# Clustered attention and two MLPs on one core: operands of the first head pair written by ACT and DVE, centroids masked, the first scores split, idle matmuls placed

## The chip, the cores and the metric

One core of a Trainium2 chip. The metric is the device time of one execution in microseconds (us). PE is TensorE, DVE is VectorE, ACT is ScalarE, POOL is GpSimd, SP is SyncE, which here only issues DMAs.

## What is computed

```python
# q, k, v: (2 batches, 8 heads, 768 tokens, 64); centroids: (8, 16, 64)
q_assign = argmax(q_n @ c_n.T)          # nearest of 16 centroids, by cosine
k_assign = argmax(k_n @ c_n.T)
mask   = q_assign[..., :, None] == k_assign[..., None, :]
scores = where(mask, 0.125 * q @ k.T, -1e9)
attn   = softmax(scores)
x = (attn @ v) reshaped to (1536, 512)
x = max(max(x @ w1, x @ w2), x @ w3) @ w_out      # width 768
h = x @ w_in;  out = max(0.01 * h, h) @ w_out2    # width 2048
```

## The kernel before

Attention runs first, then both MLPs. The 16 heads of the two batches are taken as 8 pairs; a pair's q and k stand transposed in SBUF as 128 x 768 (`rq`, `rk`, head 0 in partitions 0 to 63, head 1 in 64 to 127). A unit is 256 query rows of one head, six units a pair, 48 in all.

Every float32 product is made from a high part (rounded to fp32r) and a low rest. For one head the score operands are four tiles: q1 holds the high part of q over its low part, k1 the high part of k twice, q2 the high part of q over 16 rows that tell q's cluster, k2 the low part of k over 16 rows that hold 0 or -2^100 by k's cluster. The sum q1.k1 + q2.k2 is then the masked score. In `scores` (L534) 128 query rows of a unit take four matmuls at L543: two (512 and 256 columns) with q1 and k1 over 128 rows, two with q2 and k2 over 80 rows, all into one of two PSUM buffers. `maxima` (L548) is the row maximum on DVE, `exps` (L553) the exponential with its row sum on ACT; after it the PSUM buffer is free. `transposes` (L585, L593) turns the exponentials on PE, `out_of_psum` and `rests` split them, `values` (L627, L638) multiplies them by v.

For a pair's operands `round_q` and `round_k` (L380, L385) write the high parts of both heads in one 128-row tile, `rest_q` and `rest_k` (L390, L395) the low ones, and `operands` (L500, L504) copies half tiles by DMA on SP's queue into q1, q2, k1, k2: six copies a head, each 64 x 768, and two small ones for the cluster rows. Clusters come from `sims` (L417, L421: six products of 128 tokens with 32 centroid columns, twelve matmul records), `near_max`, `near_eq`, `weigh`, `first_max` and `first_eq` (L432 to L472: five short steps on DVE that give a one-hot of the first maximum), and a transposition of the one-hot on PE: `onehot_T` (L479), or for head 0 of the first pair `onehot_up` (L488), from where CQ (L849, ACT) and CK (L854 on DVE, then L857 on ACT) bring the 16 rows into q2 and k2.

The order of every engine's work is written out by hand. `BEGIN` (L53) is a list of steps that is emitted first, `ORDER` (L37) the six lists that repeat for the units, `END` (L60) the last. A step "S0:1" is score half 0 of unit 1, "G0@1" the q side of `sims` for pair 1, "I2" is `idle(WARM[2])`. `idle(n)` (L786) emits n bf16 matmuls of 128 x 512 zeros into a PSUM tile that nothing reads. WARM is (8, 2, 3, 4): 8 at the start, 2 after the centroids' transposition, 3 at I2.

The beginning, with what the steps stand for: load centroids, rq, rk; scale the centroids to length one and write the result twice side by side (L809), transpose (L811), copy the two 64 x 64 halves into `cb` that was cleared before (L794, L814), so that a pair's head 0 meets only its own 16 columns and head 1 its own; G0@0, G1@0 (clusters of pair 0), G0@1, UQ, idle, G1@1, UK, CK; S0:0, S1:0 (the first scores); OT (one-hots for head 1), S0:1, S1:1, T0:0 and so on. D0a and D0b are the DMA copies of heads 0 and 1 of pair 0; D2 is head 1's cluster rows.

Of the kernel before, what the change touches and what calls it, by code (L numbers as in the profile page):

```python
# [8 lines left out]
F32 = mybir.dt.float32  # L9
# [8 lines left out]
P = 128  # L18
# [32 lines left out]
)  # L51

BEGIN = (  # L53
# [4 lines left out]
)  # L58

END = (  # L60
# [13 lines left out]
}  # L74
WAYS = ("DPP", "DDP", "DPA", "DDP", "DDP", "DPA")
ENGINE = {"QH": "A", "QH@1": "P", "KH": "P", "VH": "P", "KL": "P", "KL@0": "D", "VL": "P", "W": "P", "W@1": "D"}
WARM = (8, 2, 3, 4)
PACE = 0.16
FIRST = ("G0", "G1", "N0a", "N0b", "N1a", "N1b", "W", "QH", "KH", "QL", "LD")
SPARE = {"G0": (4, 0), "G1": (5, 0), "O0": (2, 0), "O1": (3, 0)}  # L80
# [7 lines left out]
def clustered_attention_mlps(  # L88
# [229 lines left out]
    with ExitStack() as att:  # L318
# [92 lines left out]
        def bank():  # L411

            st["bank"] = st.get("bank", -1) + 1
            ps = ps_s.tile([P, 1024], F32, tag="s", name=f"s{st['bank']}")
            return ps[:, 0:S], ps[:, S:1024]
# [84 lines left out]
        def operands(p, part, heads=(0, 1), queue=nc.sync):  # L500
# [5 lines left out]
            for j in heads:  # L506
# [12 lines left out]
                else:  # L519
# [3 lines left out]
                    if part != 1:  # L523
                        dma(q2[D : D + C], s["oo"][j * C : (j + 1) * C])
                        dma(k2[D : D + C], s["oo"][(2 + j) * C : (3 + j) * C])

        un = {}

        def unit(n):
# [1 line left out]
            j, g = divmod(r, NG)  # L531
            return p, j, g

        def scores(n, i):  # L534
            p, j, g = unit(n)
            q1, q2, k1, k2 = st[p][j]
            if i == 0:
                un[n] = {"e": [], "sum": sums[n % len(sums)]}
            c0 = g * G + i * P
            ps, spare = bank()  # L540
            for a, b, start in ((q1, k1, True), (q2, k2, False)):
                for lo, hi in ((0, 512), (512, S)):
                    nc.tensor.matmul(  # L543
                        ps[:, lo:hi], a[:, c0 : c0 + P], b[:, lo:hi], start=start, stop=not start
                    )
            un[n]["s", i], un[n]["spare", i] = ps, spare

        def maxima(n, i):  # L548
            mx = sm.tile([P, 1], F32, tag="mx", name=f"mx{n}_{i}", bufs=4)
# [146 lines left out]
        def do(op, at):  # L696

            o, d = op[:-1], op[-1]
            d = int(d) if d.isdigit() else 0
            if op == "LD":  # L700
                load_pair(at)
            elif op == "QH":
                round_q(at)
            elif op == "KH":
                round_k(at)
            elif op == "QL":
                rest_q(at)
            elif op == "KL":
                rest_k(at)
            elif op == "VH":  # L710
                split_v(at, 0)
            elif op == "VL":
                split_v(at, 1)
            elif o == "G":
                sims(at, d, spare(at, op, 2))
            elif op[0] == "N":
                j = int(op[1])
                if op[2] == "a":
                    near_max(at, j, spare(at, f"G{j}", 2))
                else:  # L720
                    near_eq(at, j)
            elif op == "W":
                weigh(at, nc.gpsimd if engine("W", at) == "P" else nc.vector)
            elif op == "FA":
                first_max(at)
            elif op == "FB":
                first_eq(at)
            elif o == "O":
                onehot_T(at, d, spare(at, op, 1))
            elif op == "SP":  # L730
                spread(at)
            elif o == "P":
                penalties(at, d, spare(at, f"O{d}", 1))
            elif o == "D":
                operands(at, 3 * d)
            elif o == "S":
                scores(at, d)
            elif o == "M":
                maxima(at, d)
            elif o == "X":  # L740
                exps(at, d)
            elif op == "RA":
                guard(at)
            elif op == "RC":
                inverse(at)
            elif op == "RB":
                if unit(at)[1] == 1:
                    widen(at)
            elif o == "T":
                transposes(at, d)  # L750
            elif o == "E1":
                out_of_psum(at, d, "copy" if way(at, d) == "P" else "hi")
            elif o == "E2":
                if way(at, d) == "A":
                    out_of_psum(at, d, "copy")
            elif o == "B":
                if way(at, d) == "P":
                    his(at, d)
            elif o == "L":
                rests(at, d)  # L760
            elif o == "V":
                values(at, d)
            elif op == "Y":
                move(at)
            elif op == "K1":
                keep(at)
            elif op == "K2":
                scale(at)
            else:
                raise ValueError(op)  # L770

        pieces, scraps = {}, {}
        if True:
# [12 lines left out]
            def idle(n):  # L786
                for _ in range(n):
                    nc.tensor.matmul(warm, nought[:, 0:P], nought, start=True, stop=True)  # L788
# [2 lines left out]
            make_identity(nc, idf)  # L791
            nc.gpsimd.memset(half, 0.5)
            nc.vector.tensor_copy(idb, idf)
            nc.vector.memset(cb, 0.0)  # L794
            nc.vector.memset(gain[0 : 2 * C], 1.0)
            nc.vector.memset(gain[2 * C : 4 * C], BIG)
            nc.vector.memset(gain[D : D + C], BIG)
# [7 lines left out]
            nc.gpsimd.tensor_tensor(sq, sq, half, op=ALU.pow)  # L805
            nc.vector.tensor_scalar_add(sq, sq, 1e-6)
            nc.vector.reciprocal(sq, sq)
            for j in range(2):
                nc.vector.tensor_scalar_mul(cn[:, j, :], ct, sq)  # L809
            cps = ps_t.tile([P, P], F32, tag="t", name="cps")  # L810
            nc.tensor.transpose(cps, cn.rearrange("p j d -> p (j d)"), idf)  # L811
            for j in range(2):
                r = slice(j * D, (j + 1) * D)
                nc.vector.tensor_copy(  # L814
                    cb[r, :, j * C : (j + 1) * C],
                    cps[r].rearrange("p (n j c) -> p n j c", j=2, c=C)[:, :, j, :],
                )
            idle(WARM[1])

            oh0 = sm.tile([P, D + NQ * 4 * C], BF16, tag="oh", name="oh0", bufs=1)  # L820
# [5 lines left out]
            def start(op):  # L826

                if op[0] == "I":
                    idle(WARM[int(op[1])])
                elif op in ("D0a", "D0b"):  # L830
                    for part in range(2):
                        operands(0, part, ("ab".index(op[2]),))
                elif op == "D2":
                    operands(0, 2, (1,))
                elif op == "LD1":
                    load_pair(1, "qk", nc.scalar)
                elif op in ("LV0", "LV1"):
                    load_pair(int(op[2]), "v")
                elif op in ("Wq", "Wk"):
                    weigh(0, nc.vector, "qk".index(op[1]))  # L840
                elif op in ("FAq", "FAk"):
                    first_max(0, "qk".index(op[2]))
                elif op in ("FBq", "FBk"):
                    first_eq(0, "qk".index(op[2]))
                elif op in ("UQ", "UK"):
                    onehot_up(0, "QK".index(op[1]), scrap(op))
                elif op == "CQ":
                    ps = scrap("UQ").bitcast(BF16)[D : D + C, 0:S]
                    nc.scalar.copy(st[0][0][1][D : D + C], ps)  # L849
                elif op == "CK":  # L850
                    ps = scrap("UK").bitcast(BF16)[D : D + C, 0:S]
                    to, n = st[0][0][3][D : D + C], S // 2
                    up = slice(D, D + C)
                    nc.vector.tensor_scalar(  # L854
                        to[:, 0:n], ps[:, 0:n], BIG, -BIG, op0=ALU.mult, op1=ALU.add
                    )
                    nc.scalar.activation(  # L857
                        to[:, n:], ps[:, n:], AF.Identity, scale=gain[up], bias=base[up]
                    )
                elif op == "OT":  # L860
                    for h in range(2):
                        onehot_T(0, h, scrap(op)[:, 256 * h : 256 * h + 256])
                elif op in ("PA", "PB"):
                    h = "AB".index(op[1])
                    penalties(0, h, scrap("OT")[:, 256 * h : 256 * h + 256])
                elif op == "in":
                    until_scores.close()
                    open_inputs()
                elif op == "ph":
                    until_exps.close()  # L870
                    open_products()
                    st["first"] = hidden(0, 0)
                elif op == "h":
                    next(st["first"])
                elif op[0] == "x":
                    split_x(0, (int(op[1]),))
                else:
                    take_apart(op)
# [111 lines left out]
```

## Time and profile before

| | |
|---|---|
| runs | 720.86, 725.62, 725.58 us; median 725.58 |
| profiled execution | 726.17 us, of which the span of its instructions is 724.3 |
| PE busy | 709.7 us of the span (98%), by far the most |
| mean granted clock | 0.982 of 2.4 GHz |

The rows further down come from the profiled execution; times in them count from the first instruction. The engine columns give busy time and, as x, the count of instructions. The matmul records show a duration that overlaps the next one's, so the pace of a stretch of matmuls is the distance of their starts; the chain view shows that distance.

### The profile page before, as it was taken

The numbers are of one execution on the slowest core, as the hardware profiler recorded it, in microseconds if no ns is written. First come the engines' busy times: TensorE is split into PE (matmuls) and PEld (weight loads), VectorE is DVE, ScalarE is ACT, GpSimd is POOL, SyncE is SP. The second block draws the span as 40 slices with busy tenths as digits, with TensorE's granted clock in tenths as the row PEclk, the third lists the DMA queues.
The fourth block names the chain that finished last, engine by engine and source line by source line (L and its number), as shares of the span: only waits on it lengthen the run. The fifth ranks groups of instructions, "written<-read, shape, count | busy, mean of one in ns | idle before, by whom it ended". The sixth has DMA issues, their size and how long they took to land.

```text
span 724.3 us, 10793 instructions
## 1 busy us (share of the span) xinstructions
PE 709.7 (98%) x3866; PEld 609.0 (84%) x3866; DVE 531.7 (73%) x1009; ACT 374.0 (52%) x718; POOL 285.7 (39%) x264
## 2 busy tenths in 40 slices
PE   9899999999999999999999999999999999999997
PEld 6799898889889988888888888888888888888886
DVE  4778989899988868988887299779619945983222
ACT  1678888888889965532222034446433433432220
POOL 2578797878878741111110111223212322312220
PEclk7599999999999999999999999999999999999999
DMA  8795281956343003755545045416505531510112
GB/s 219 186 273 127 90 219 49 235 139 172 100 114 88 1 1 108 270 175 173 161 148 187 0 146 176 145 60 201 178 27 154 183 128 48 184 58 1 44 43 88
DMA packets 30150, 92.37 MB, mean 128 GB/s; under 512 B 4528, under 2 KB 4528, under 8 KB 30096
## 3 DMA queue, kind: packets, MB, share of 16 engines
q1 hardware_dynamic: 29808, 90.89, 42.0%
q10 hardware_dynamic: 288, 0.79, 0.4%
q8 instruction: 31, 0.51, 0.3%
q14 instruction: 23, 0.19, 0.1%
HBM read 68.16 MB, written 3.15 MB: 98 GB/s over the span
## 4 chain that ended last, share of the span: by engine, by line
PE 86%; DVE 6%; ACT 3%; DMA 2%; issue 2%; POOL 1%; SPq 0%; ACTq 0%; POOLq 0%; DVEq 0%
PE h L245 13%; PE h L247 13%; PE h L246 13%; PE y L247 8%; PE y L245 8%; PE y L246 8%; PE s L543 7%; PE o L638 6%; PE t L593 6%; DVE mx L550 2%; PE s L421 2%; PE scrap L421 1%; DVE el L622 1%; PE warm L788 1%; DMA k<-oo 1%
## 5 line engine op out<-in xcount | busy, mean ns | idle before, releaser
L279 POOL TENSOR_TENSOR hl<-a,hh 128x512 fp32r<-128x512 f32 x66 | 91.8, 1391 | 344.3 <-ACT hh L278 344.3
L245 PE MATMUL h<-xh,wh 128*128 128x512 f32 x408 | 159.1, 390 | 0.0
L246 PE MATMUL h<-xl,wh 128*128 128x512 f32 x408 | 158.9, 390 | 0.1
L247 PE MATMUL h<-xh,wl 128*128 128x512 f32 x408 | 158.8, 389 | 0.0
L550 DVE TENSOR_REDUCE mx<-s 128x1 f32<-128x768 f32 x96 | 91.4, 952 | 22.2 <-PE s L543 10.7
L278 ACT CAST hh<-a 128x512 fp32r<-128x512 f32 x66 | 41.1, 623 | 124.6 <-DVE a L272 73.8
L245 PE MATMUL y<-hh,wh 128*128 128x512 f32 x264 | 102.7, 389 | 0.0
L246 PE MATMUL y<-hl,wh 128*128 128x512 f32 x264 | 102.7, 389 | 0.0
L247 PE MATMUL y<-hh,wl 128*128 128x512 f32 x264 | 102.7, 389 | 0.0
L625 POOL TENSOR_TENSOR el<-et,eh 128x512 fp32r<-128x512 f32 x72 | 98.6, 1377 | 3.1 <-ACT et L610 0.2
L543 PE MATMUL s<-k,q 128*128 128x512 f32 (+3 forms) x384 | 93.7, 368 | 6.2 <-ACT ee L556 3.2
L556 ACT ACTIVATE ee<-s,mx 128x768 f32<-128x768 f32 x96 | 87.0, 906 | 16.2 <-DVE mx L550 15.3
L246 PEld LDWEIGHTS h<-xl,wh 128*128 128x128 f32 x408 | 76.6, 188 | 16.6 <-DVE xl L236 0.8
L247 PEld LDWEIGHTS h<-xh,wl 128*128 128x128 f32 x408 | 76.6, 188 | 15.9
L245 PEld LDWEIGHTS h<-xh,wh 128*128 128x128 f32 x408 | 76.6, 188 | 15.7
L270 ACT COPY a<-h 128x512 f32<-128x512 f32 x66 | 38.6, 585 | 93.3 <-PE h L247 91.8
L593 PE MATMUL t<-idf,ee 128*128 128x128 f32 x576 | 80.5, 280 | 1.8 <-DVE rs L566 1.4
L305 DVE TENSOR_TENSOR acc<-y,acc 128x512 f32<-128x512 f32 x72 | 48.6, 685 | 40.5 <-PE y L247 40.5
L274 DVE SCALAR_TENSOR_TENSOR a<-a,h 128x512 f32<-128x512 f32 x48 | 32.8, 684 | 61.7 <-ACT a L270 61.6
L638 PE MATMUL o<-eh,vs 128*128 128x256 f32 x288 | 74.0, 290 | 0.0
L543 PEld LDWEIGHTS s<-k,q 80*128 80x128 f32 (+1 forms) x384 | 61.9, 200 | 13.9 <-ACT ee L556 4.4
L638 PE MATMUL o<-el,vs 128*128 128x256 f32 x288 | 72.3, 283 | 0.0
(101 smaller groups left out, 1163.4 us busy)
## 6 DMA issues: line engine op xcount, KB each, us to landing
raw<-in_w SPq DMA_DIRECT2D x56, 512.0 KB, 4.1
low<-in_w SPq DMA_DIRECT2D x56, 511.5 KB, 3.5
q<-qh SPq DMA_DIRECT2D x32, 192.0 KB, 4.9
k<-kh SPq DMA_DIRECT2D x32, 192.0 KB, 4.7
q<-ql SPq DMA_DIRECT2D x16, 192.0 KB, 4.7
k<-kl SPq DMA_DIRECT2D x16, 192.0 KB, 3.8
rv<-in_v SPq DMA_DIRECT2D x8, 384.0 KB, 5.9
out_T<-acc SPq DMA_DIRECT2D x12, 256.0 KB, 2.0
```

The source lines that it names most:

```text
L245: nc.tensor.matmul(ps, ah, bh, start=(k == 0), stop=False)
L246: nc.tensor.matmul(ps, ah, bl, start=False, stop=False)
L247: nc.tensor.matmul(ps, al, bh, start=False, stop=(k == n - 1))
L278: nc.scalar.copy(hh[:, f, :], a)
L279: nc.gpsimd.tensor_tensor(hlo[:, f, :], a, hh[:, f, :].bitcast(F32), op=ALU.subtract)
L305: nc.vector.tensor_tensor(a, ps, a, op=ALU.add)
L543: nc.tensor.matmul(ps[:, lo:hi], a[:, c0 : c0 + P], b[:, lo:hi], start=start, stop=not start)
L550: nc.vector.tensor_reduce(mx, un[n]["s", i], axis=AX.X, op=ALU.max, negate=True)
L556: nc.scalar.activation(e, u.pop(("s", i)), AF.Exp, bias=u.pop(("m", i)), scale=1.0, accum_out=u["sum"][:, i, 0:1],)
L593: nc.tensor.transpose(ps[:, kk, i * P : (i + 1) * P], u["e"][i][:, (k + kk) * P : (k + kk + 1) * P], idf,)
L625: nc.gpsimd.tensor_tensor(lo, et, hi.bitcast(F32), op=ALU.subtract)
L638: nc.tensor.matmul(u["o"], vs[:, t, :], u[e][:, t, :], start=(t == 0 and e == "eh"), stop=(t == NQ - 1 and e == "el"),)
```

## The change

WARM becomes (8, 4) and a number behind I is now the count of idle matmuls: four after the centroids' transposition, two behind G0@0, G1@0, G0@1 and S0:2, one before the second pass of the first scores, four before T0:1. The q and k load of pair 1 and the v load of pair 0 are issued from ACT's queue. Steps Z write the operands of pair 0 straight from `rq` and `rk`, 64 rows at a time: for each head ACT writes the high part of q to q1 (q) and again to q2 (r), of k to the two halves of k1 (k, j), and DVE writes the low parts into q1 (l) and k2 (m). KH@0, QH@0, QL@0, KL@0, D0a and D0b are gone. CK is one ACT instruction. G1@1 stands behind the first scores.

```diff
 BEGIN = (
-    "KH@0 QH@0 LD1 G0@0 QL@0 G1@0 KL@0 D0a G0@1 N0a@0 N0b@0 Wq FAq FBq UQ CQ I2 G1@1 N1a@0 N1b@0 Wk FAk FBk "
-    "UK CK S0:0 M0:0 S1:0 X0:0 M1:0 OT LV0 D0b X1:0 N0a@1 N0b@1 N1a@1 N1b@1 S0:1 M0:1 PB PA D2 S1:1 T0:0 "
-    "VH@0 VL@0 QH@1 KH@1 M1:1 X0:1 X1:1 T2:0 LV1 T4:0 W@1 S0:2 E10:0 M0:2 FA@1 S1:2 E12:0 FB@1 X0:2 M1:2 "
-    "L0:0 E14:0 B2:0 L2:0 LD@2 T0:1 O0@1 P0@1 QL@1 X1:2"
+    "Zaq LDq Zal Zak LDk Zaj Zam G0@0 I2 G1@0 Zar I2 N0a@0 N0b@0 Wq FAq FBq Zbq UQ Zbk CQ LV0 G0@1 I2 N1a@0 "
+    "N1b@0 Wk FAk FBk Zbl UK CK Zbr Zbj SA0:0 SA1:0 Zbm I1 SB0:0 M0:0 SB1:0 X0:0 M1:0 G1@1 OT X1:0 N0a@1 "
+    "N0b@1 N1a@1 N1b@1 S0:1 M0:1 PB PA D2 S1:1 T0:0 VH@0 VL@0 QH@1 KH@1 M1:1 X0:1 X1:1 T2:0 LV1 T4:0 W@1 "
+    "S0:2 E10:0 M0:2 FA@1 I2 S1:2 E12:0 FB@1 X0:2 M1:2 L0:0 E14:0 B2:0 L2:0 LD@2 I4 T0:1 O0@1 P0@1 QL@1 X1:2"
 )
...
-WARM = (8, 2, 3, 4)
+WARM = (8, 4)
...
+        def first_operands(j, what):
...
+            q1, q2, k1, k2 = s[j]
+            rq, rk = (s[x][j * D : (j + 1) * D] for x in ("rq", "rk"))
+            if what == "q":
+                rounded("A", q1[0:D], rq, SCALE)
+            elif what == "r":
+                rounded("A", q2[0:D], rq, SCALE)
+            elif what == "k":
+                rounded("A", k1[0:D], rk)
+            elif what == "j":
+                rounded("A", k1[D:P], rk)
+            elif what == "l":
+                rest("D", q1[D:P], rq, q1[0:D], SCALE)
+            else:
+                rest("D", k2[0:D], rk, k1[0:D])
...
-        def scores(n, i):
+        def scores(n, i, parts=(0, 1)):
...
+            elif o in ("SA", "SB"):
+                scores(at, d, ("AB".index(o[1]),))
...
-            nc.vector.memset(cb, 0.0)
+            one = sm.tile([P, 2, 1], F32, tag="one", name="one", bufs=1)
+            nc.vector.tensor_reduce(
+                one, idf.rearrange("p (n j c) -> p j n c", j=2, c=C), axis=AX.XY, op=ALU.add
+            )
...
-            for j in range(2):
-                nc.vector.tensor_scalar_mul(cn[:, j, :], ct, sq)
+            nc.vector.scalar_tensor_tensor(
+                cn, ct.rearrange("p (o d) -> p o d", o=1).to_broadcast([P, 2, D]), sq,
+                one.to_broadcast([P, 2, D]), op0=ALU.mult, op1=ALU.mult,
+            )
...
-            for j in range(2):
-                r = slice(j * D, (j + 1) * D)
-                nc.vector.tensor_copy(
-                    cb[r, :, j * C : (j + 1) * C],
-                    cps[r].rearrange("p (n j c) -> p n j c", j=2, c=C)[:, :, j, :],
-                )
+            nc.vector.tensor_copy(cb.rearrange("p n c -> p (n c)"), cps)
...
-                    nc.vector.tensor_scalar(
-                        to[:, 0:n], ps[:, 0:n], BIG, -BIG, op0=ALU.mult, op1=ALU.add
-                    )
                     nc.scalar.activation(
-                        to[:, n:], ps[:, n:], AF.Identity, scale=gain[up], bias=base[up]
+                        st[0][0][3][up], ps, AF.Identity, scale=gain[up], bias=base[up]
                     )
```

## Rows read from the trace of the kernel before

**Rows 1.** The page: busy time, the granted clock in 40 slices, and the chain.
```profile
PE 709.7 (98%) x3866; PEld 609.0 (84%) x3866; DVE 531.7 (73%) x1009; ACT 374.0 (52%) x718; POOL 285.7 (39%) x264
PEclk7599999999999999999999999999999999999999
PE 86%; DVE 6%; ACT 3%; DMA 2%; issue 2%; POOL 1%; SPq 0%; ACTq 0%; POOLq 0%; DVEq 0%
```
**Rows 2.** Busy by stretch: PE, PEld, DVE, ACT, POOL; granted clock; DMA share; GB/s.
```profile
1.17:5.94 4.77, 4.77 (x12) 1.60 (x13) 2.70 (x38) 1.67 (x2) 1.45 (x4) 1.00 0.64 208
5.94:9.36 3.42, 3.42 (x33) 3.42 (x32) 3.25 (x7) 0.00 (x0) 0.12 (x1) 1.00 1.02 280
9.36:26.42 17.06, 16.45 (x71) 13.82 (x71) 8.11 (x16) 7.49 (x14) 4.77 (x5) 0.50 0.75 177
26.42:29.84 3.42, 1.71 (x13) 1.23 (x11) 3.06 (x5) 2.05 (x5) 1.95 (x3) 1.00 0.87 245
29.84:36.66 6.82, 6.69 (x27) 5.80 (x28) 5.59 (x9) 3.92 (x9) 4.74 (x5) 0.50 1.03 240
36.66:60.00 23.34, 23.34 (x186) 22.20 (x186) 18.34 (x39) 19.66 (x41) 16.81 (x19) 1.00 0.76 225
```
**Rows 3.** The chain up to 41 us: start, duration, what.
```profile
1.17 3.59 PE warm L788 x8
...
5.18 0.85 PE warm L788 x2
6.04 4.49 PE scrap L421 x36
10.52 0.65 PE scrap L488 x6
...
12.46 2.40 PE scrap L421 x12
...
15.55 0.57 DVE k L854
...
16.14 0.67 ACT k L857
...
19.93 2.93 PE s L543 x8
22.86 1.72 PE t L593 x8
...
37.81 0.71 PE s L543 x4
38.52 1.26 PE s L421 x12
```
**Rows 4.** Timeline of DVE: start, duration, line, operation, out<-in, [idle before].
```profile
5.81 1.05 DVE L375 SCALAR_TENSOR_TENSOR ql<-rq,qh 128x768 fp32r<-128x768 f32 x1
...
9.32 0.36 DVE L472 TENSOR_TENSOR oh<-e,m 128x192 bf16<-128x192 f32 x1
...
17.90 0.96 DVE L550 TENSOR_REDUCE mx<-s 128x1 f32<-128x768 f32 x1 [1.80 <-PE s L543]
...
32.12 0.96 DVE L550 TENSOR_REDUCE mx<-s 128x1 f32<-128x768 f32 x1
...
37.81 0.42 DVE L663 TENSOR_TENSOR acc<-o,tmp 64x256 f32<-64x256 f32 x1 [1.55 <-ACT tmp L657]
```
**Rows 5.** Timeline of ACT, the same columns.
```profile
4.18 0.84 ACT L367 ACTIVATE qh<-rq 128x768 fp32r<-128x768 f32 x1 [2.18 <-DMA rq<-in_qT]
...
11.21 0.79 ACT L849 CAST q<-scrap 16x768 fp32r<-16x768 bf16 x1 [6.19 <-PE scrap L488]
...
18.89 0.90 ACT L556 ACTIVATE ee<-s,mx 128x768 f32<-128x768 f32 x1 [2.09 <-DVE mx L550]
...
38.33 0.91 ACT L556 ACTIVATE ee<-s,mx 128x768 f32<-128x768 f32 x1
```
**Rows 6.** Timeline of SP: the copy of k's low part for head 0 of pair 0.
```profile
9.57 0.86 SPq L504 DMA_DIRECT2D k<-kl  x1
```
**Rows 7.** DMA issues of the first 40 us: count, size, median us to landing.
```profile
k<-kl SPq DMA_DIRECT2D x4, 192.0 KB, 5.1
```

More of the change, by code (lines that the diff above doesn't have):

```diff
@@ L525, in operands @@
                         dma(k2[D : D + C], s["oo"][(2 + j) * C : (3 + j) * C])
+        def first_operands(j, what):
+            s = st[0]
+            if j not in s:
+                s[j] = tuple(
+                    opn.tile([D + C if x[1] == "2" else P, S], F32R, tag=x, name=f"{x}_0_{j}")
+                    for x in ("q1", "q2", "k1", "k2")
+                )
[13 more added lines that the diff above has]
+                rest("D", k2[0:D], rk, k1[0:D])
         un = {}
@@ L532, in unit @@
             return p, j, g
-        def scores(n, i):
+        def scores(n, i, parts=(0, 1)):
             p, j, g = unit(n)
             q1, q2, k1, k2 = st[p][j]
-            if i == 0:
+            if n not in un:
                 un[n] = {"e": [], "sum": sums[n % len(sums)]}
             c0 = g * G + i * P
-            ps, spare = bank()
-            for a, b, start in ((q1, k1, True), (q2, k2, False)):
+            if 0 in parts:
+                un[n]["s", i], un[n]["spare", i] = bank()
+            ps = un[n]["s", i]
+            for part in parts:
+                a, b, start = ((q1, k1, True), (q2, k2, False))[part]
                 for lo, hi in ((0, 512), (512, S)):
@@ L545, in scores @@
                     )
-            un[n]["s", i], un[n]["spare", i] = ps, spare
         def maxima(n, i):
@@ L807, in clustered_attention_mlps @@
             nc.vector.reciprocal(sq, sq)
-            for j in range(2):
-                nc.vector.tensor_scalar_mul(cn[:, j, :], ct, sq)
+            nc.vector.scalar_tensor_tensor(
+                cn, ct.rearrange("p (o d) -> p o d", o=1).to_broadcast([P, 2, D]), sq,
+                one.to_broadcast([P, 2, D]), op0=ALU.mult, op1=ALU.mult,
+            )
             cps = ps_t.tile([P, P], F32, tag="t", name="cps")
             nc.tensor.transpose(cps, cn.rearrange("p j d -> p (j d)"), idf)
-            for j in range(2):
-                r = slice(j * D, (j + 1) * D)
-                nc.vector.tensor_copy(
-                    cb[r, :, j * C : (j + 1) * C],
-                    cps[r].rearrange("p (n j c) -> p n j c", j=2, c=C)[:, :, j, :],
-                )
+            nc.vector.tensor_copy(cb.rearrange("p n c -> p (n c)"), cps)
             idle(WARM[1])
@@ L828, in start @@
                 if op[0] == "I":
[L829 to L832, printed above, removed]
+                    idle(int(op[1:]))
+                elif op[0] == "Z":
+                    first_operands("ab".index(op[1]), op[2])
                 elif op == "D2":
                     operands(0, 2, (1,))
-                elif op == "LD1":
-                    load_pair(1, "qk", nc.scalar)
+                elif op in ("LDq", "LDk"):
+                    load_pair(1, op[2], nc.scalar)
                 elif op in ("LV0", "LV1"):
-                    load_pair(int(op[2]), "v")
+                    load_pair(int(op[2]), "v", (nc.scalar, nc.sync)[int(op[2])])
                 elif op in ("Wq", "Wk"):
@@ L851, in start @@
                     ps = scrap("UK").bitcast(BF16)[D : D + C, 0:S]
-                    to, n = st[0][0][3][D : D + C], S // 2
                     up = slice(D, D + C)
-                    nc.vector.tensor_scalar(
-                        to[:, 0:n], ps[:, 0:n], BIG, -BIG, op0=ALU.mult, op1=ALU.add
-                    )
                     nc.scalar.activation(
-                        to[:, n:], ps[:, n:], AF.Identity, scale=gain[up], bias=base[up]
+                        st[0][0][3][up], ps, AF.Identity, scale=gain[up], bias=base[up]
                     )
```

## The prediction

> **What bounds the kernel now.** I read the page first: PE is busy for 98% of the span and holds 86% of the chain that ended last [rows 1]. The line of the granted clock is full in all slices but the first two, 0.7 and 0.5. So the kernel is bound by PE, and only its beginning is not at full clock. The change edits the beginning alone. The second view, busy time by stretch, places it [rows 2]: the clock is granted at 0.50 from 9.36 to 26.42 and again from 29.84 to 36.66 us, 23.9 us together, in which PE is busy for 16.45 + 6.69 = 23.1 us. From 36.66 on PE is busy all the time at 1.00 (23.34 of 23.34 us up to 60). Whatever lets PE reach that point earlier therefore moves the end by as much; whatever does not is lost. Were PE the only bound before 36.66, full clock would save half of 23.1, 11.6 us; that is the ceiling of the clock's part.
>
> The third view, the chain, shows what half clock costs [rows 3]: twelve records of a cluster product take 2.40 us at 12.46 and 1.26 at 38.52; eight records of scores take 2.93 us at 19.93, four take 0.71 at 37.81, so eight would take 1.42. The first stretch, 1.17 to 5.94, is listed at 1.00, but its eight idle matmuls of 512 columns take 3.59 us, and the next two 0.85, 0.43 each: 1.2 GHz, the lower level.
>
> What the clock follows can be read too. It fell at 9.36 although PE was busy for 3.42 of 3.42 us [rows 2]: in that stretch PE did nothing but cluster products, 32 columns wide [rows 3]. It fell at 29.84 after a stretch with PE busy for half of it, 1.71 of 3.42. It rose at 26.42 after scores and transpositions without a gap. And at 38.52 twelve of the same products, standing between scores and transpositions, did not bring it down. So small products in a long row lose the clock, and mixed with wide matmuls they can keep it.
>
> **The change part by part, if the clock holds.** *Preamble.* Five short DVE instructions (one clear, two scalings, two copies) become three. The nearest row is a step of 0.36 us [rows 4]: a gain of 0 to 0.7. I take nothing, because the products stand behind four idle matmuls instead of two: 0.43 more at full clock, 0.85 at half. The first product begins at about 6.4 instead of 6.04.
>
> *Operands.* Per head four ACT and two DVE instructions over 64 rows replace two roundings, two rests and six copies. A narrower tile is not cheaper here: on ACT 16 rows take 0.79 and 128 rows 0.84 us [rows 5]. I take 0.84, and 1.0 on DVE, where 128 rows take 1.05 and 64 rows of a third of the width 0.42 [rows 4]; half of 1.05 and three times 0.42 are the ends. DVE's first two (Zal, Zam) take the place of QL and KL, so its ten cluster steps begin as before, 0.1 late at most: FBq ends at 9.8 instead of 9.68, FBk at 11.75. ACT's first six run from 4.18 to 9.4, before CQ is ready: free.
>
> *PE up to UK.* 6.4 + 1.26 = 7.7; two idle, 8.1; G1@0, 9.4; two idle, 9.85; UQ 0.35 (half of 0.65 [rows 3]), 10.2; G0@1, 11.5; two idle, 11.95; UK 0.4, 12.4. Before, UK ended at 15.5: 3.1 us later, 2.4 of it the product G1@1 that now stands behind the first scores.
>
> *CK and the first scores.* Two instructions in a row, 0.57 and 0.67, become one of 768 columns: between 0.79 [rows 5] and twice 0.67; I take 1.0, so CK runs from 12.5 to 13.6. The first pass of both scores (0.71) lies under it, since its operands are ready at about 7.2. The second pass gives DVE the first score at 14.3 instead of 17.90 [rows 4]. Were the copies still there, the last one for head 0, issued at 9.57 for 0.86 [rows 6] and landing 5.1 later [rows 7], would be next at about 15.5; so the copies, hidden before, are worth 1.9 us only beside the other edits. Queued behind the waits: on ACT CK is followed by Zbr and Zbj, to 15.3, and then by the first exponential, which waits for the maximum (14.3 + 0.96) until 15.3 anyway; on DVE Zbl and Zbm fill 11.75 to 13.8 and leave 0.5 us to spare. If an instruction is 0.3 longer than I take it, that much shows. The exponential begins at 15.35 instead of 18.89 [rows 5]: -3.5. The v load on ACT's queue goes out at about 11.3, some 0.8 later than before, and is first used at 26.
>
> *From there to 36.66.* Score tiles turn over by maximum and exponential now, no longer by half-speed scores. Exponentials stand at 15.35, 16.25, 18.65 and 19.55 (four cluster steps of DVE, 1.55 us, lie between); the scores of unit 2 at 19.7 and, behind two idle, 20.9; their maxima at 20.65 and, behind two steps of pair 1's clusters (0.55 each, an estimate from 0.36 at half the width [rows 4]), 22.6; P0@1 until 24.0, then unit 3: its first maximum at 25.25 instead of 32.12 [rows 4], -6.9; its second exponential at 29.5 instead of 38.33 [rows 5], -8.8. By then PE has no gaps left, as before from 36.66 on. The extra idle matmuls lie inside these times or in PE's waits.
>
> *Sum.* -3.5 to the first exponential, -3.4 to unit 3's first maximum, -1.9 to its second exponential: -8.8. The profiled execution took 726.17 us (span 724.3 and 1.9 around it): 717.4. The median of the runs, 725.58, is 0.6 below it: 716.8. I say 717.0. The open prices (preamble -0.7 to +0.5, CK -0.2 to +0.3, the DVE writes -0.5 to +0.3 each, of which little shows) give 715.5 to 719.
>
> **The rivals.** *The clock falls at about 9.4 all the same.* Twelve products with two idle matmuls between is less wide work than the surroundings at 38.52, more than the 36 in a row; no row lies between, so this is near an even chance. Then from 9.4 at half clock: idle 10.3, UQ 11.0, G0@1 13.4, idle 14.3, UK 15.0, first pass 16.4, idle and second pass 18.3, G1@1 20.7, one-hots 21.5 (0.8, an estimate from 0.65 for as many in UQ), four scores 24.4, where before they ended at 22.86: 1.5 late. But the second half-clock stretch would not come, as PE is then behind and idle matmuls fill its gaps: half of 6.69, -3.35. Net -1.9: 724.
>
> *The clock holds at first and falls later,* between 20 and 26, where PE still waits (0.9 us for P0@1). One half-clock stretch like that at 29.84 stays: -8.8 + 3.35 = -5.4, 721.
>
> The Trainium skill bears on both, in TensorE: Matmul & The Clock Gate. Its section "Why this matters for your kernels" asks for no long idle gaps of PE; by that rule the clock would hold here and the first rival would have hardly a chance. The trace differs: it fell at 9.36 with PE busy throughout [rows 2], so I keep that rival. The section "Part 4: PE-mode transpose" says that transposes don't count as PE being busy; by it the second rival would be likely, 721. The trace speaks against it: the clock rose after a row of transpositions and scores [rows 2, 3].
>
> *The other side: the idle matmuls cost more than they bring.* This decides if the clock does not come up at about 6 at all, as could be when the first burst falls otherwise in time. The 36 products, 4.49 before, cost 7.2 at half clock, +2.7; eleven idle matmuls before unit 1's scores instead of five, +2.6; less 0.3 of waits. That is +5.0, less 3.35 if the second fall is bridged: 728; if it is not, 731.
>
> **How the numbers follow.** Forecast 0.45; early fall 0.25; later fall 0.13; other side 0.12; none of these 0.05. The range 715 to 728 leaves out some 2 in 10; the forecast's own is 715.5 to 719. Three runs of before lie 4.8 us apart, so the clock may step differently from run to run, and a median of few runs may mix the cases. A difference of 1% (7.3 us) is about what a measurement of this kernel can tell from no change. Under 718.3: five sixths of the forecast and a few hundredths of the rest, 0.42. Over 732.8: 0.04. Between: 0.54.
>
> **What would show it.** Right: granted clock 1.00 from about 6 us on, UK at about 12, first maximum at 14.3, second exponential of unit 3 at 29.5, and the same length as before from there on. An early fall shows as 0.50 from about 9.4 and UK at 15; a later one as 0.50 somewhere from 20 to 30; the other side as cluster products of 2.4 us from the first on. The forecast is also wrong if the first maximum comes on time and the gain is gone by 60 us, which would mean that DMAs or DVE, not PE, bound the stretch behind.

## The result and the profile after

The changed kernel takes 716.70 us, median of 6 runs (715.36 to 719.13), beside 725.18 for 6 runs of before (720.86 to 729.28): a ratio of 0.9899, 95% interval 0.9873 to 0.9925. The forecast was 717.0 and -8.8 us. The profiled execution took 716.41 us, its span is 714.6, 9.7 less than before's. One run of no_idle further down (728.26 us at a mean granted clock of 0.984) was in a slower state and is left out of that kernel's median and range.

The page of the kernel after, the lines of [rows 1]:

```profile
PE 702.6 (98%) x3878; PEld 602.0 (84%) x3878; DVE 532.0 (74%) x1008; ACT 379.9 (53%) x725; POOL 285.4 (40%) x263
PEclk9999999999999999999999999999999999999999
PE 86%; DVE 6%; ACT 3%; DMA 1%; issue 1%; POOL 1%; SPq 0%; ACTq 0%; DVEq 0%; POOLq 0%
```

PE has twelve records more and is busy 7.1 us less: the same products, and twelve more idle ones, at a faster clock. The two dark slices of the clock line, 7 and 5, are gone. Busy time by stretch says where, in the columns of [rows 2]:

```profile
1.17:5.94 4.77, 4.77 (x12) 1.70 (x13) 2.79 (x36) 1.98 (x3) 0.73 (x3) 1.00 0.57 180
5.94:7.18 1.24, 1.24 (x7) 0.93 (x4) 1.21 (x2) 1.22 (x2) 0.00 (x0) 1.00 0.83 277
7.18:16.00 8.82, 8.73 (x73) 7.38 (x72) 7.06 (x15) 6.34 (x9) 2.22 (x2) 1.00 0.26 93
16.00:26.42 10.42, 9.56 (x66) 7.21 (x66) 9.37 (x16) 9.26 (x20) 6.98 (x7) 1.00 0.48 135
26.42:29.84 3.42, 3.42 (x29) 3.25 (x27) 2.73 (x7) 3.29 (x8) 2.98 (x4) 1.00 1.05 273
29.84:36.66 6.82, 6.82 (x59) 6.66 (x59) 4.37 (x12) 5.62 (x12) 5.87 (x6) 1.00 1.04 239
```

Before, the two stretches at 0.50 (9.36 to 26.42 and 29.84 to 36.66) had 71 and 27 PE records; now the 6.82 us from 29.84 hold 59. And the DMA share between 7 and 16 us is 0.26, where before every row from 5.94 to 36.66 stood at 0.75 to 1.03 [rows 2]: the twelve copies are gone. The chain of the kernel after, with the durations from start to start:

```profile
5.09 1.71 PE warm L815 x4
6.80 1.50 PE scrap L421 x12
...
10.42 0.42 PE scrap L488 x6
10.84 1.31 PE scrap L421 x12
...
12.59 0.35 PE scrap L488 x6
...
12.96 0.98 ACT k L880
...
16.74 1.85 PE s L569 x8
18.59 1.31 PE t L618 x12
```

Twelve records of a cluster product take 1.31 where they took 2.40 [rows 3], eight of scores 1.85 (with a wait in it) instead of 2.93. The four idle matmuls still take 0.43 each: up to about 7 us PE is at its lower level, 1.2 GHz, although the stretch is listed at 1.00, as before. Then DVE and ACT, the lines that answer to [rows 4, 5]:

```profile
5.58 0.95 DVE L375 SCALAR_TENSOR_TENSOR q<-rq,q 64x768 fp32r<-64x768 f32 x1
...
8.34 0.36 DVE L432 TENSOR_REDUCE m<-scrap 128x12 f32<-128x192 f32 x1 [0.83 <-PE scrap L421]
...
14.65 1.82 DVE L575 TENSOR_REDUCE mx<-s 128x1 f32<-128x768 f32 x2 [0.45 <-PE s L569]
...
19.50 0.55 DVE L452 TENSOR_TENSOR e<-e,desc 128x384 f32<-128x384 f32 x1
...
22.31 0.56 DVE L472 TENSOR_TENSOR oh<-e,m_None 128x384 bf16<-128x384 f32 x1
...
25.59 0.96 DVE L575 TENSOR_REDUCE mx<-s 128x1 f32<-128x768 f32 x1
```

```profile
15.69 0.90 ACT L581 ACTIVATE ee<-s,mx 128x768 f32<-128x768 f32 x1
...
29.65 0.91 ACT L581 ACTIVATE ee<-s,mx 128x768 f32<-128x768 f32 x1
```

| step | before | predicted | after |
|---|---|---|---|
| first maximum | 17.90 | 14.3 | 14.65 |
| first exponential | 18.89 | 15.35 | 15.69 |
| first maximum of unit 3 | 32.12 | 25.25 | 25.59 |
| second exponential of unit 3 | 38.33 | 29.5 | 29.65 |

At the last of them the changed kernel is 8.68 us ahead. In the two timelines it is 8.68 ahead at the exponential that starts at 86.57 and 9.1 at the last one (246.02 instead of 255.12): between these two executions, what is won in the first 30 us is kept.

### The profile page after: what moved, and what is told of

It is laid out like the page before. It is cut to its first block, busy times and chain, and to the rows that moved or that the text cites. A ratio compares the mean times of both kernels' runs of the same rounds, so it can differ in the third digit from the quotient of the medians.

```text
span 714.6 us, 10798 instructions
## 1 busy us (share of the span) xinstructions
PE 702.6 (98%) x3878; PEld 602.0 (84%) x3878; DVE 532.0 (74%) x1008; ACT 379.9 (53%) x725; POOL 285.4 (40%) x263
## 4 chain that ended last, share of the span: by engine, by line
PE 86%; DVE 6%; ACT 3%; issue 1%; DMA 1%; POOL 1%; SPq 0%; ACTq 0%; DVEq 0%; POOLq 0%
PE h L247 13%; PE h L245 13%; PE h L246 13%; PE y L246 8%; PE y L247 8%; PE y L245 8%; PE s L569 6%; PE o L663 6%; PE t L618 6%; DVE mx L575 2%; PE s L421 2%; PE warm L815 1%; ACT ee L581 1%; DVE el L647 1%; DVE wx L166 1%
## 5 line engine op out<-in xcount | busy, mean ns | idle before, releaser
L569 PE MATMUL s<-k,q 128*128 128x512 f32 (+3 forms) x384 | 89.6, 354 | 5.3 <-ACT ee L581 3.2
L581 ACT ACTIVATE ee<-s,mx 128x768 f32<-128x768 f32 x96 | 87.0, 907 | 11.1 <-DVE mx L575 10.2
L618 PE MATMUL t<-idf,ee 128*128 128x128 f32 x576 | 78.3, 275 | 1.8 <-DVE rs L591 1.4
L569 PEld LDWEIGHTS s<-k,q 80*128 80x128 f32 (+1 forms) x384 | 58.6, 190 | 12.7 <-ACT ee L581 4.6
```

What stands on the lines that cost most here:

```text
L569: nc.tensor.matmul(ps[:, lo:hi], a[:, c0 : c0 + P], b[:, lo:hi], start=start, stop=not start)
L581: nc.scalar.activation(e, u.pop(("s", i)), AF.Exp, bias=u.pop(("m", i)), scale=1.0, accum_out=u["sum"][:, i, 0:1],)
L618: nc.tensor.transpose(ps[:, kk, i * P : (i + 1) * P], u["e"][i][:, (k + kk) * P : (k + kk + 1) * P], idf,)
```

## The experiments

Theory 1: most of the gain is PE's clock, which the idle matmuls hold; the other edits clear the way for it and add a little. Rival: the gain is the earlier first scores, by operands and order. Each kernel has six runs, no_idle five, copies_back twelve, beside before on the same chip; not all were on one chip, so a ratio compares better than a time. The last three columns are of the profiled execution, which is one of the runs and seldom the median one (the slowest of old_idle and g1_early, the fastest of no_idle_early, unsplit, warm2 and mask_back): first maximum, second exponential of unit 3, and the time listed at 0.50 in the first 40 us.

| kernel | us, median (range) | ratio to before | first max. | unit 3 | at 0.50 |
|---|---|---|---|---|---|
| before | 725.18 (720.86 to 729.28) | 1 | 17.90 | 38.33 | 23.9 |
| after | 716.70 (715.36 to 719.13) | 0.9899 | 14.65 | 29.65 | 0 |
| after_again | 717.62 (716.27 to 720.75) | 0.9894 | 14.60 | 29.61 | 0 |
| old_idle | 719.24 (717.85 to 722.96) | 0.9917 | 17.00 | 34.59 | 6.8 |
| no_idle | 719.84 (717.46 to 721.72) | 0.9920 | 16.14 | 32.79 | 10.2 |
| no_idle_early | 719.50 (716.98 to 723.67) | 0.9920 | 14.11 | 29.13 | 3.4 |
| no_idle_late | 717.32 (716.13 to 719.81) | 0.9889 | 13.65 | 28.44 | 0 |
| copies_back | 723.69 (719.66 to 727.12) | 0.9968 | 16.06 | 33.52 | 3.4 |
| unsplit | 718.75 (717.00 to 720.66) | 0.9905 | 14.40 | 29.60 | 0 |
| warm2 | 717.44 (715.62 to 720.52) | 0.9884 | 13.94 | 28.93 | 0 |
| g1_early | 720.73 (718.98 to 720.97) | 0.9922 | 14.75 | 31.61 | 3.4 |
| more_idle | 718.27 (717.45 to 721.33) | 0.9902 | 15.75 | 31.18 | 0 |
| mask_back | 718.32 (716.55 to 721.39) | 0.9898 | 13.99 | 29.01 | 0 |
| best | 718.36 (715.65 to 719.20) | 0.9891 | 13.78 | 28.73 | 0 |

The 95% intervals of the ratios are some 0.0035 to each side (0.9882 to 0.9953 for old_idle, 0.9882 to 0.9957 for no_idle, 0.9947 to 0.9989 for copies_back), so kernels within about 2 us of each other are not told apart by their times; for these the profile is read. The mean granted clock of every run is known too. The time ahead of the first rise counts in it as 1.00; behind that rise, 0.999 or 1.000 leaves no room for a stretch of 3.4 us at 0.50, which alone gives 0.998.

**old_idle**: the idle matmuls alone, in the kernel of before.

```diff
-WARM = (8, 2, 3, 4)
+WARM = (8, 4)
-    "... G0@0 QL@0 G1@0 KL@0 D0a G0@1 ... CQ I2 G1@1 ... S0:2 ... FA@1 S1:2 ... LD@2 T0:1 ..."
+    "... G0@0 I2 QL@0 G1@0 I2 KL@0 D0a G0@1 I2 ... CQ G1@1 I2 ... S0:2 ... FA@1 I2 S1:2 ... LD@2 I4 T0:1 ..."
```

> The old kernel with the idle matmuls alone: four behind the centroids' transposition, two behind each of the four cluster products, two and four around unit 2's scores. Operands still by DMA copies, CK in two instructions, scores in one pass, G1@1 ahead of the first scores. Theory 1 (most of the gain is the clock that the idle matmuls hold): granted clock 1.00 from 6 to 8 us on, first maximum at 16 to 17, 717.5 to 720 us, 0.990 to 0.993 of before. Rival (the gain is the earlier first scores, by operands and order; idle matmuls are not what counts): 724 to 728, as before or slower, since ten idle matmuls are added.

Measured 719.24, 6.4 below before: as theory 1 said, and against the rival. (It has 13 idle matmuls more than before, not the ten of the expectation.) In its profile the clock stayed up from 3.98 to 17.64. Two views of it, PE's timeline and busy time by stretch:

```profile
15.22 0.59 PE L543 MATMUL s<-k,q 128*128 128x512 f32 x2 [1.93 <-DMA q<-ql]
```

```profile
17.64:24.46 6.82, 6.21 (x28) 5.58 (x28) 4.98 (x9) 5.45 (x12) 4.25 (x4) 0.50 0.70 151
```

With PE early, the copies are what the first scores wait for: PE stood idle for 1.93 us until the copy of q's low part landed, and behind that gap the clock fell for 6.8 us. That the gap is the reason is not shown. This profile is of the slowest of its six runs, 722.96 us at a mean clock of 0.995; the five others, 717.85 to 719.77, have 0.999 or 1.000, so no such fall. The idle matmuls alone, then, mostly hold the clock in the old kernel too.

**no_idle, no_idle_early, no_idle_late**: the changed kernel without all I steps, without the early ones, without the two around unit 2's scores.

```diff
-    "... G0@0 I2 G1@0 Zar I2 ... G0@1 I2 ... SA1:0 Zbm I1 SB0:0 ... FA@1 I2 S1:2 ... LD@2 I4 T0:1 ..."
+    "... G0@0 G1@0 Zar ... G0@1 ... SA1:0 Zbm SB0:0 ... FA@1 S1:2 ... LD@2 T0:1 ..."
```

> The changed kernel without the idle matmuls of steps I (the twelve at the start and behind the transposition stay). Theory 1: the clock falls to 0.50 around 9 to 11 us and comes back at about 26 or later; first maximum at about 16, 721 to 726 us. Rival: 715 to 717, no slower than the changed kernel, as twenty idle matmuls less are in PE's way.

> The changed kernel without the idle matmuls between the cluster products and the first scores; the six late ones stay. Theory 1: clock falls at 9 to 11 us, back at about 26, then held: 721 to 724 us. Rival: 715 to 716.5.

> The changed kernel without the six idle matmuls around unit 2's scores; the early ones stay. Theory 1: the clock is held up to about 20 us, then may fall once in the stretch with PE's waits (21 to 25): 716 to 717 where it does not, 719 to 721 where it does. Rival: 715.5 to 716.5 in every run.

Measured 719.84, 719.50 and 717.32. (The steps I hold 13 idle matmuls, not the twenty of the expectation.) The rival of the first two is out by their medians, and theory 1 missed as well: both come out below its ranges, as the clock fell where it had it, but came back much sooner. Busy time by stretch of no_idle, then its chain:

```profile
6.59:10.00 3.41, 2.74 (x26) 2.63 (x24) 2.77 (x7) 3.23 (x4) 0.00 (x0) 1.00 0.41 124
10.00:16.83 6.83, 6.83 (x35) 6.34 (x35) 4.24 (x8) 3.45 (x4) 2.87 (x3) 0.50 0.20 59
16.83:27.07 10.24, 8.74 (x60) 6.78 (x61) 9.13 (x16) 9.26 (x19) 4.90 (x6) 1.00 0.50 129
27.07:30.48 3.41, 3.41 (x16) 3.22 (x16) 2.59 (x8) 2.39 (x6) 2.97 (x2) 0.50 0.97 255
```

```profile
10.86 2.51 PE scrap L421 x12
...
14.02 2.72 PE s L569 x8
```

It fell at 10.00 after the cluster products, and rose at 16.83 after the eight score records of the first two scores, which now stand in one piece from 14.02 to 16.74. Why here is open: before, eight such records stood without a gap from 19.93 to 22.86 [rows 3], and the clock rose only at 26.42. So the other edits shorten the time at half clock by themselves, in these profiles from 23.9 to 10.2 us. no_idle_early fell at 10.85 and rose at 14.26; that profile is of its fastest run (716.98 at a mean clock of 0.997), and its five others have 0.988 to 0.998. Without the late idle matmuls nothing changed that the medians can tell, though 717.32 lies a little above both forecasts; the profile shows the clock up throughout, and the start of unit 3's scores no later. One of its six runs, 719.81 at a mean clock of 0.995, lost the clock somewhere, as theory 1 allowed.

**copies_back**: the changed kernel with operands by roundings, rests and DMA copies.

```diff
-    "Zaq LDq Zal Zak LDk Zaj Zam G0@0 I2 ... Zar ... Zbq ... Zbk ... Zbl ... Zbr Zbj ... Zbm ..."
+    "KH@0 QH@0 LDq LDk G0@0 QL@0 KL@0 D0a I2 ... M1:0 D0b G1@1 ..."
```

> The changed kernel with pair 0's operands by roundings, rests and the twelve DMA copies again; mask, split scores, order and idle matmuls stay. Theory 1 (the copies are next in line once PE is early): the last copy of head 0 for the first pass lands at about 15.2, the first pass starts there instead of 12.7, first maximum at 16.3 to 17, PE idle for some 2 us before it, 718 to 721 us. Rival (the copies are hidden anyway): first maximum at 14.7, 716 to 717.5 us.

Measured 723.69, slower than theory 1 had it. PE's timeline, DVE's and POOL's, then POOL's in the changed kernel:

```profile
14.50 0.94 PE L569 MATMUL s<-k,q 128*128 128x512 f32 x4 [1.83 <-DMA q<-ql]
...
25.46 0.35 PE L479 MATMUL s<-idb,oh 128*64 128x128 bf16 x3 [0.90 <-DVE oh L472]
```

```profile
20.86 1.22 DVE L452 TENSOR_TENSOR e<-e,desc 128x384 f32<-128x384 f32 x1
...
24.09 1.31 DVE L472 TENSOR_TENSOR oh<-e,m_None 128x384 bf16<-128x384 f32 x1
```

```profile
18.13 0.83 POOL L370 TENSOR_SCALAR vs<-rv 128x768 fp32r<-128x768 f32 x1 [11.95 <-DMA rv<-in_v]
```

```profile
13.70 1.20 POOL L370 TENSOR_SCALAR vs<-rv 128x768 fp32r<-128x768 f32 x1 [9.97 <-DMA rv<-in_v]
```

The wait for the copy costs 1.36 us at the first exponential (17.05 instead of 15.69). The rest comes behind it. The v load is issued from ACT's queue as in the changed kernel (10.64 and 10.88), but beside the copies it takes 7.4 us to land instead of 2.7, so POOL's four steps on v, q and k begin at 18.13 instead of 13.70 and run beside DVE's cluster steps of pair 1, which take 1.22 and 1.31 instead of 0.55 and 0.56; PE waits 0.90 us for these before unit 3, and the clock falls at 27.09 for 3.4 us. At unit 3's second exponential it is 3.87 behind. Part of the rest goes with the clock: of its twelve runs the five at a mean clock of 0.997 or 0.998 take 719.66 to 722.67 us, the four at 0.987 or 0.988 724.80 to 727.12.

**unsplit, g1_early, mask_back**: one edit undone each.

```diff
-    "... CK Zbr Zbj SA0:0 SA1:0 Zbm I1 SB0:0 M0:0 SB1:0 X0:0 ..."
+    "... CK Zbr Zbj Zbm S0:0 M0:0 S1:0 X0:0 ..."
```

> The changed kernel with the first two scores each in one piece (no first pass ahead of CK for the second score) and without the idle matmul between. Theory 1: the first score loses nothing, the second 0.35 us of PE that lies under the first maximum; first maximum at 14.6, 716 to 717.5 us. Rival (the split carries part of the gain): first maximum 0.35 or more later, 717.5 to 718.5 us.

```diff
-    "... G0@1 I2 N1a@0 ... M1:0 G1@1 OT ..."
+    "... G0@1 I2 G1@1 N1a@0 ... M1:0 OT ..."
```

> The changed kernel with the fourth cluster product (G1@1) ahead of UK again. Theory 1: behind the first scores it lies where PE would wait for the first exponential; ahead of UK it delays UK and the first maximum by its 1.26 us, to about 15.9: 717.5 to 718.5 us. Rival (PE bounds this stretch, so its place is the same): 716 to 717 us.

```diff
+            nc.vector.memset(cb, 0.0)
-            nc.vector.tensor_reduce(one, ...)
...
-            nc.vector.scalar_tensor_tensor(cn, ...)
-            nc.vector.tensor_copy(cb.rearrange("p n c -> p (n c)"), cps)
+            for j in range(2):
+                nc.vector.tensor_scalar_mul(cn[:, j, :], ct, sq)
...
+                nc.vector.tensor_copy(cb[r, :, j * C : (j + 1) * C], ...)
```

> The changed kernel with the centroids of before: cleared tile, two scalings, two copies. Theory 1: the first cluster product stands behind the four idle matmuls, which end 0.7 us or more after the centroids are there, so nothing shows: first cluster product and first maximum within 0.1 of the changed kernel's, 716 to 717.5 us. Rival: 0.3 us later and 717 to 718.

unsplit shows the exponentials at the same places as the changed kernel (29.60 and 29.65 at unit 3, 112.10 and 112.16 at the 41st): the split is worth nothing there. Its profile is of its fastest run (717.00); where its median, 2 us above after's and 1.1 above after_again's, comes from is not shown (four of its six runs have a mean clock of 0.998). g1_early comes out at 720.73, more than expected; its clock came up early, at 3.99, which by itself puts the first maximum about 1 us earlier (13.65 in no_idle_late, up at 4.76), and against that kernel it has it 1.10 later, near the 1.26 of theory 1; then the clock fell from 17.64 to 21.06. mask_back, up at 4.78, is compared with no_idle_late as well. DVE's first operand step in both:

```profile
5.71 0.95 DVE L375 SCALAR_TENSOR_TENSOR q<-rq,q 64x768 fp32r<-64x768 f32 x1
```

```profile
5.49 0.95 DVE L376 SCALAR_TENSOR_TENSOR q<-rq,q 64x768 fp32r<-64x768 f32 x1
```

The second is no_idle_late's, with the mask: 0.22 earlier, and 0.34 at the first maximum. So the mask brings 0.3 us where the clock comes up early, against theory 1's 0.1; where DVE waits for PE (0.83 us in the profile after) it should bring nothing, which no run shows. The times can't tell: 718.32 lies above both forecasts.

**warm2, more_idle**: two idle matmuls instead of four behind the transposition; four instead of two behind the early products and before S1:2.

```diff
-WARM = (8, 4)
+WARM = (8, 2)
```

> The changed kernel with two idle matmuls behind the centroids' transposition instead of four. Theory 1: in the profile of the changed kernel DVE waited 0.83 us for the first cluster product, so the first maximum comes 0.8 earlier, at about 13.9, where the clock comes up as early: 715.5 to 716.5 us. Rival: the shorter first burst misses the clock's rise in part of the runs; these take 720 us or more and the median is 717 to 720.

```diff
-    "... G0@0 I2 G1@0 Zar I2 ... G0@1 I2 ... FA@1 I2 S1:2 ..."
+    "... G0@0 I4 G1@0 Zar I4 ... G0@1 I4 ... FA@1 I4 S1:2 ..."
```

> The changed kernel with four idle matmuls where it has two behind the three early cluster products and before unit 2's second score. Theory 1 (two are enough to hold the clock): only their price shows, 0.43 us for each pair that lies on PE's path, first maximum at 15.1 to 15.6, 717 to 718.5 us. Rival (two are not enough in part of the runs): median and highest run fall, 715.5 to 716.5.

warm2 has the first maximum 0.71 earlier and stays 0.72 to 0.83 ahead to the last exponential, with the clock up at 6.67; its median, 717.44, is above theory 1's range and not told apart from after's (ratios 0.9884 and 0.9899). more_idle pays 1.10 us at the first maximum and 1.53 at unit 3, and gains no steadiness: its highest run is 721.33, at a mean clock of 0.995.

**after_again and best**: the changed kernel again, and one that joins warm2 with an earlier penalty step and has two idle matmuls instead of four at T0:1.

```diff
-WARM = (8, 4)
+WARM = (8, 2)
-    "... L0:0 E14:0 B2:0 L2:0 LD@2 I4 T0:1 O0@1 P0@1 QL@1 X1:2"
+    "... L0:0 B2:0 L2:0 LD@2 O0@1 P0@1 T0:1 I2 E14:0 X1:2"
+    ONCE: (1, 12): "QL@1"
```

> The changed kernel once more, beside the three others on one chip: 715.5 to 718.5 us.

> The changed kernel with two idle matmuls behind the transposition instead of four, with pair 1's one-hots and penalties ahead of T0:1 and of ACT's copy of T4:0, and QL@1 behind unit 3's first maximum. Theory 1: first maximum 0.7 earlier (13.95) and PE's wait for the penalties 0.5 shorter, 715 to 716.3 us. Rival: the work put off is next in line and nothing is won behind the first maximum, 716 to 717.5.

best is 0.92 ahead of the changed kernel at unit 3, 1.08 at the 41st exponential, and 0.9 behind at the last. By its time, 718.36, it beats neither the changed kernel nor warm2, and misses both forecasts. Of the 1.7 us that its lead lost by the 51st exponential, 0.9 is a row of PE's timeline, which after_again has too. In order, best, after_again and after:

```profile
131.62 0.59 PE L571 MATMUL s<-k,q 80*128 80x512 f32 x2 [1.43 <-DMA k<-oo]
```

```profile
132.44 0.58 PE L569 MATMUL s<-k,q 80*128 80x512 f32 x2 [1.23 <-DMA k<-oo]
```

```profile
131.78 0.59 PE L569 MATMUL s<-k,q 80*128 80x512 f32 x2 [0.51 <-DMA q<-oo]
```

Here the first scores of pair 4 wait for the copies of its cluster rows, which still go by DMA. no_idle_late waits 1.83 us in this place and turns a lead of 1.20 into 0.96 behind. after_again equals after to 0.06 us up to the 41st exponential and is 4.2 behind at the end: 1.5 from this place, 2.3 across a fall of the clock at 184.55, the rest by 200 us. Busy time by stretch of after_again:

```profile
184.55:187.96 3.41, 3.41 (x18) 3.41 (x18) 1.89 (x3) 1.82 (x4) 0.58 (x1) 0.50 0.05 19
```

The changed kernel's own profile has 29 PE records at 1.00 in these 3.41 us. This is the scatter that hides edits below 2 us.

## Why the prediction was right

**The bound and the ceiling.** PE bounds everything behind the beginning, and the shift at the last predicted step, -8.68, is carried to the end of attention (-9.1). That view held for these two profiles; in others part of a lead went at the DMA wait at 131 us.

**The clock.** In the profiled execution it was held from 7.18 us on, the case given 0.45. Two of the six runs (718.28 and 719.13) have a mean clock of 0.997, so some 4 us at half clock (an estimate: twice 0.003 of 717); where, no profile shows. What the rows of before could not say, whether two idle matmuls behind twelve narrow products are enough, the runs say: with them it stayed up beyond 16 us in each of the eight profiles that have them with engine-written operands and G1@1 behind the scores (after, after_again, no_idle_late, unsplit, warm2, mask_back, more_idle with four each, best), without them it fell at 10.00 and 10.85. The section "Why this matters for your kernels" of TensorE: Matmul & The Clock Gate in the Trainium skill puts falls of the clock down to long idle gaps of PE. The traces do not bear that out: old_idle lost the clock behind a gap of 1.93 us, shorter than the gaps that the section names, and no_idle lost it at 10.00 with PE busy for 2.74 of the 3.41 us before, most of it on narrow products; the measurement decides.

**Sizes.** To the first exponential -3.20 against -3.5: the first product began at 6.80, not 6.4, because the upper level came at about 7.2 in this execution and not at 5.94, so the four idle matmuls were paid at 0.43 each. That is the term that was off; by it DVE's cluster steps begin 0.58 late (8.34 instead of 7.76 before), where the prediction had 0.1 at most. CK took 0.98 (1.0 said), DVE's 64-row steps 0.95 (1.0), ACT's 0.84. From there to unit 3's first maximum -3.33 (-3.4), to its second exponential -2.15 (-1.9).

**What was attributed wrongly.** The copies were priced at 1.9 us beside the other edits. At the first exponential they cost 1.36, but in time 5 to 7 (by the ratios, 0.9968 against 0.9899, and by the medians, 723.69 against 716.70, which may not be of one chip). The step that failed is taking a wait for its own length. Behind it the v load, slower beside the copies, moves POOL's work onto DVE's; the prediction had v first used at 26, but POOL takes it up as it lands, at 13.70 in the changed kernel. And the clock falls more often, though that PE's gap brings this about is inferred. The rival of an early fall, 724, was too dear for the changed kernel without its idle matmuls: it kept PE at half clock until 24.4 at least, but with the other edits this ends at 16.83 (719.84).

**The split of the gain.** The idle matmuls alone bring 6.4 us, everything else alone 5.8 (725.6, the runs of before beside them, less 719.24 and 719.84), both together 8.5 to 8.8. So the other edits add 2.1 to 2.4 on top of the idle matmuls, but are worth more than theory 1's little without them. The two do not add because both shorten the same half-clock time: 23.9 us before, 10.2 without idle matmuls, none in the profile with both and, by the mean clock, none in five of the six runs with idle matmuls alone. Shown are the half-clock stretches; that they are the whole of the overlap is inferred. Not tried by themselves are CK in one instruction and the v load on ACT's queue (pair 1's q and k load stood there before). Not settled is when the clock comes up or falls in a given execution: the first rise lay between 3.98 and 7.18 us in these profiles, and with it the first maximum between 13.65 and 14.65 for nearly the same code.

## What to carry to other kernels

Where PE bounds, look first for stretches below full clock: there PE's work takes about twice as long (2.40 us against 1.26 for a cluster product here), and a few wide idle matmuls between narrow products, here 13, can bring more than removing work. A step that looks hidden, here twelve copies, may be next in line and then cost several times its wait. Read small edits by a fixed step early in the timeline and not by the total, which scatters by 4 us here.

## What was not expected of the hardware

DVE's two-input steps on SBUF took twice as long beside POOL: 128x384 at 1.22 and 1.31 us in copies_back against 0.55 with POOL idle and 0.56 where DVE's step began just ahead of POOL's in the changed kernel. SBUF — State Buffer in the Trainium skill, under "Who interferes with whom", says that a DVE instruction with two SBUF inputs contends with a POOL instruction that reads SBUF; these rows agree. And a short fall of the clock, 3.4 us at 0.50, appeared at 184.55 in after_again and at 184.9 in g1_early, in the middle of attention where every other profile has 1.00.
